# The product with v ahead of the sinks' transposes in the bank that they share

## The chip, the cores and the metric

The kernel runs on one core of a Trainium2 chip. The metric is the device time of one execution in microseconds (us). A difference is read as a ratio of medians of several runs.

## What is computed

Sliding-window attention with a few "sink" keys, a LayerNorm with a two-layer network behind it, and a token-mixing stage. Two batches, 8 heads, 768 positions, head width 64; the window is 128 keys and the first 4 keys are sinks.

```python
scores = scale * np.matmul(q, k.transpose(0, 1, 3, 2))
keep = is_sink | in_window                       # pos < n_sink, or 0 <= rel < window
scores = np.where(keep, scores, -1000000000.0)
a = np.exp(scores - np.max(scores, axis=-1, keepdims=True))
a = a / (np.sum(a, axis=-1, keepdims=True) + 1e-09)
attn = np.matmul(a, v)
...
xn = (x - mu) / np.sqrt(var + 1e-06) * g_ln
x = x + np.maximum(xn @ w_ch1, 0.0) @ w_ch2
...
theta = x @ w_theta
y = einsum('ts,bsd->btd', w_tok_r, x * cos(theta)) + einsum('ts,bsd->btd', w_tok_i, x * sin(theta))
u = x + y
out = u + np.maximum(u @ w_ch, 0.0)
```

## The kernel before

The 1536 positions of both batches are cut into six pieces of 256 (two tiles of 128 rows). Pieces 0 to 2 are batch 0, pieces 3 to 5 batch 1. Attention goes piece by piece and head by head; the network (`first`, line L625, and `second`, line L651) goes in 56 units, each for one slice of 128 hidden columns and for the one or two pieces that are active then. The work of TensorE (PE) is issued exactly in the order in which the program writes it; the other engines' instructions are put in order by the scheduler of the language, which also places the waits. `run` writes the network's units and calls `advance` between their parts, which takes the next few steps of the attention generator `attn_fast`. So PE's one queue holds parts of the network with attention steps between them, and none of it can be passed by another.

One step of `attn_fast` (one head of one piece) writes on PE, in this order:

- the scores of both tiles, each into a bank of its own (L274, L275 or L278); behind them VectorE (DVE) adds the mask (L381) and ScalarE (ACT) takes the exponential (L384), into the tile `p`;
- `turn_w` (L397), for the head one step back: three or four 128x128 transposes of `p` into a bank `wp`, which ACT (L400) and DVE (L401) read out as the two fp16 parts of `wt`;
- `finish`, which takes one more bank, named `pv`, for two unrelated things. `turn_sinks` (L410) transposes the 16 sink columns of the head that `turn_w` has just turned into columns 256 to 511; ACT (L411) and DVE (L412) read them out as the two parts of the tile `ws`. `values` (L426) multiplies the `wt` and `ws` of the head before that with v into columns 0 to 127, and DVE (L441, `normalize`) reads the result into `x`.

The sinks are turned only for pieces that do not begin a batch: 1, 2, 4 and 5, so in 32 of the 48 steps. The `ws` that `values` reads was written one whole step earlier (three `ws` tiles go round). During most of the attention the banks go round among three, and a step takes four, so a bank comes back after three more tiles.

Names in what follows: `h` is the bank of `first`, `hh` (ACT, L629) and `hl` (DVE, L630) its two parts; `acc` are the banks of `second`; `wh` (ACT, L593) and `wl` (GpSimd, POOL, L594) the parts of a weight; `xn` the normalised rows and `tp` (L571) their transposes at the end of a piece; L502 to L506 unpack the 64-bit weights.

Of the kernel before, what the change touches and what calls it, by code (L numbers as in the profile page):

```python
# [71 lines left out]
class Net:  # L72
# [207 lines left out]
    def attn_fast(self, eng):  # L280

        steps = [(piece, h) for piece in range(NP) for h in range(H)]
        nc, p, qk, pending, turned, late = self.nc, self.att, {}, [], [], []

        def load(j, eng=eng):
            if j < len(steps):
                piece, h = steps[j]
                if piece >= STACKED:
                    qk[piece, h] = self.stack_qk(piece, h, nc.gpsimd)
                elif h % 2 == 0:  # L290
                    qk[piece, h] = qk[piece, h + 1] = self.split_qk(piece, h // 2, eng)

        def load_v(piece):
            if piece < NP:
                b, tiles = self.tiles(piece)
                for t in tiles + ([NT] if tiles[-1] >= 2 else []):
                    self.split_v(b, t)

        def first_of_all(piece):
            return self.ahead() if piece == 0 else ExitStack()  # L300

        def turn():

            piece, h, pt, st = pending.pop(0)
            b, tiles = self.tiles(piece)
            with first_of_all(piece):
                wt, blocks = self.turn_w(pt, tiles)
            p["ws"].append(p["ws"].pop(0))
            turned.append((piece, h, wt, p["ws"][-1], blocks, st))
            return (pt, p["ws"][-1]) if tiles[0] else None  # L310

        def finish(sinks, ready):

            bank = self.bank("pv")
            if sinks:
                self.turn_sinks(bank, *sinks)
            if not ready:
                return
            piece, h, wt, ws, blocks, st = turned.pop(0)
            b, tiles = self.tiles(piece)  # L320
            with first_of_all(piece):
                self.values(bank, b, h, tiles, piece, wt, ws, blocks, st)
                if h % (H // 2) == H // 2 - 1:
                    self.stats(piece, h // (H // 2))
            if h == V_RANGE:
                while late:
                    q, ts = self.tiles(late.pop())
                    for t in ts:
                        with self.behind():
                            self.range_v(q, t)  # L330
            if h == H - 1:
                with first_of_all(piece):
                    self.norm(piece)
                late.append(piece)

        load(0, self.nc.vector)
        load_v(0)
        for j, (piece, h) in enumerate(steps + [(NP, 0)] * (TURN + LAG)):
            if j < len(steps):
                b, tiles = self.tiles(piece)  # L340
                if h == 0:
                    self.x[piece] = self.xp.tile([128, PIECE, DM], F32, tag=f"x{piece}", name=f"x{piece}")
                if piece < STACKED:
                    load(j + 2)
                if piece >= STACKED or h == H - 1 and piece + 1 == STACKED:
                    load(j + 1)
                if h == (3 if piece else V_NEXT):
                    load_v(piece + 1)
                pt, st = yield from self.softmax(h, tiles, qk[piece, h])
                pending.append((piece, h, pt, st))  # L350
            sinks = None
            if len(pending) > (TURN if j < len(steps) else 0):
                sinks = turn()
                yield
            ready = len(turned) > (LAG if j < len(steps) + TURN else 0)
            if sinks or ready:
                finish(sinks, ready)
                yield
        for t in tiles:
            self.range_v(b, t)  # L360
# [51 lines left out]
        nc.vector.scalar_tensor_tensor(out=ws[32:32 + NSK], in0=ps, scalar=PSC, in1=ws[0:NSK], op0=ALU.mult,  # L412
                                       op1=ALU.subtract)

    def values(self, pv, b, h, tiles, piece, wt, ws, blocks, st):

        nc = self.nc
        hc = slice(h * D, (h + 1) * D)
        for i in range(len(tiles)):
            prods = [(wt[:, x + e * len(blocks)], v[:, hc]) for e in range(2) for x, (j, t) in enumerate(blocks) if j == i  # L420
                     for v in self.v3[b, t][:2 - e]]
            if tiles[0]:
                vk = self.v3[b, NT]
                prods += [(ws[0:32 + NSK, i], vk[0:32 + NSK, 0, hc]), (ws[0:NSK, i], vk[0:NSK, 1, hc])]
            for j, (a, m) in enumerate(prods):
                nc.tensor.matmul(pv[:, i * D:(i + 1) * D], a, m, start=j == 0, stop=j == len(prods) - 1)  # L426
        self.normalize(h, pv, st, self.x[piece])

    def tiles(self, piece):
# [616 lines left out]
```

## Time and profile before

| | us |
|---|---|
| median of 3 runs (lowest to highest) | 755.43 (754.74 to 755.86) |
| the profiled execution, whole | 753.02 |
| its span in the profile | 751.2 |
| PE busy (matmuls) | 650.8 |
| DVE, ACT, POOL busy | 367.9, 365.6, 273.8 |

The profiled execution is 2.4 us shorter than the median, and 1.8 us of it lie outside the span. Attention is spread over the first 447 us of the span; from there to the end only the network's rest and the token mixing are left. A row of the trace gives what an engine did, for how long, and in brackets how long the engine had been idle before it and whose signal ended that.

### The profile page before, as it was taken

How to read it: one execution, taken by the hardware profiler on the slowest of the kernel's cores; microseconds unless marked ns; L12 is line 12 of the kernel's file. 1: busy time of each engine (PE TensorE's matmuls, PEld its weight loads, DVE VectorE, ACT ScalarE, POOL GpSimd, SP SyncE). 2: the span in 40 equal slices, each digit the busy share in tenths (PEclk: the TensorE clock that was granted, in tenths of full speed). 3: DMA queues.
4: the chain of work that ended last, by engine and by line, in shares of the span. 5: the costliest groups of instructions: out<-in, count | busy, mean ns of one | idle time of the engine just before them, and what ended most of it. 6: DMA issues, size and time to landing. Idle time of an engine off the chain costs nothing.

```text
span 751.2 us, 10135 instructions
## 1 busy us (share of the span) xinstructions
PE 650.8 (87%) x3747; PEld 523.7 (70%) x3747; DVE 367.9 (49%) x808; ACT 365.6 (49%) x774; POOL 273.8 (36%) x240
## 2 busy tenths in 40 slices
PE   3845898789889997889888889999989989899996
PEld 2633556666667675666656667778878988899996
DVE  5889624432335434353333434321367878874442
ACT  5798724344445563444434425643456656552220
POOL 3143102422437585444354117654402343330000
PEclk9999758778999998989989969999999999999999
DMA  6587401100211131110110011310011232200102
GB/s 242 185 312 262 176 20 32 30 16 0 60 31 52 44 97 40 37 38 19 37 38 1 0 57 60 123 43 0 1 31 55 85 127 71 85 15 29 37 15 82
DMA packets 19339, 50.38 MB, mean 67 GB/s; under 512 B 2769, under 2 KB 5841, under 8 KB 19281
## 3 DMA queue, kind: packets, MB, share of 16 engines
q1 hardware_dynamic: 19280, 49.66, 19.8%
q8 instruction: 31, 0.51, 0.3%
q14 instruction: 28, 0.22, 0.1%
HBM read 46.50 MB, written 3.15 MB: 66 GB/s over the span
## 4 chain that ended last, share of the span: by engine, by line
PE 38%; DVE 6%; ACT 3%; issue 1%; POOL 1%; DMA 1%; ACTq 0%; POOLq 0%; DVEq 0%
PE m L736 11%; PE h L625 8%; PE acc L651 7%; PE f L767 4%; PE th L695 4%; PE pv L426 1%; DVE st L506 1%; DVE hl L630 1%; DVE st L502 1%; DMA raw<-wtok 1%; PE tp L680 1%; DVE k L705 1%; ACT hh L629 0%; PE s L275 0%; DMA raw<-wth 0%
## 5 line engine op out<-in xcount | busy, mean ns | idle before, releaser
L594 POOL TENSOR_TENSOR wl<-w,wh 128x512 fp32r<-128x512 f32 x92 | 119.6, 1304 | 176.2 <-ACT wh L593 105.4
L625 PE MATMUL h<-xT,wh 128*128 128x512 f32 (+1 forms) x408 | 115.1, 419 | 7.6 <-DVE hl L630 7.6
L593 ACT ACTIVATE wh<-w 128x512 fp32r<-128x512 f32 x102 | 63.9, 628 | 111.0 <-PE acc L651 66.3
L625 PEld LDWEIGHTS h<-xT,wh 128*128 128x128 f32 x408 | 75.0, 210 | 27.0 <-DVE hl L630 11.2
L426 PE MATMUL pv<-v,wt 128*128 128x64 f16 x528 | 33.3, 206 | 64.9 <-DVE ws L412 55.7
L381 DVE CUSTOM_DVE_ANT_0 p<-s,mask 128x272 f32<-128x272 f32 (+1 forms) x96 | 39.4, 414 | 99.4 <-PE s L275 59.5
L651 PE MATMUL acc<-wh,hh 128*128 128x512 f32 x182 | 80.2, 441 | 0.0
L426 PEld LDWEIGHTS <-wt 128*128 128x128 f16 x528 | 26.4, 105 | 76.9 <-issue 69.0
L651 PE MATMUL acc<-wh,hl 128*128 128x512 f32 x182 | 75.1, 412 | 0.0
L651 PE MATMUL acc<-wl,hh 128*128 128x512 f32 x182 | 74.3, 408 | 0.0
L384 ACT ACTIVATE p<-p,st 128x272 f32<-128x272 f32 (+1 forms) x96 | 47.4, 494 | 51.4 <-DVE st L381 51.2
L630 DVE SCALAR_TENSOR_TENSOR hl<-h,hh 128x512 fp32r<-128x512 f32 (+1 forms) x51 | 32.1, 630 | 63.7 <-ACT hh L629 63.7
L625 PE MATMUL h<-xT,wl 128*128 128x512 f32 (+1 forms) x204 | 54.8, 394 | 0.0
L625 PEld LDWEIGHTS h<-xT,wl 128*128 128x128 f32 x204 | 39.8, 208 | 7.9
L722 POOL TENSOR_TENSOR x<-xh,xl 128x512 f32<-128x512 f32 x12 | 19.0, 1582 | 72.0 <-DVE r L716 67.2
L401 DVE SCALAR_TENSOR_TENSOR wt<-wp,wt 128x512 f16<-128x512 f32 (+1 forms) x48 | 30.7, 641 | 24.1 <-ACT wt L400 24.0
L651 PEld LDWEIGHTS acc<-wh,hl 128*128 128x128 f32 x182 | 35.9, 197 | 8.4
L651 PEld LDWEIGHTS acc<-wh,hh 128*128 128x128 f32 x182 | 35.7, 196 | 8.4
L503 ACT ACTIVATE raw<-raw 128x512 f32<-128x512 f32 (+1 forms) x52 | 36.8, 720 | 8.7 <-DVE st L502 7.6
L651 PEld LDWEIGHTS acc<-wl,hh 128*128 128x128 f32 x182 | 36.1, 198 | 5.3
L234 POOL TENSOR_TENSOR lo<-raw,hi 128x672 fp32r<-128x672 f32 (+1 forms) x11 | 18.2, 1658 | 56.4 <-ACT hi L233 56.3
L397 PE MATMUL wp<-ident,p 128*128 128x128 f32 x176 | 34.8, 322 | 2.0 <-ACT p L384 1.1
(291 smaller groups left out, 1611.2 us busy)
## 6 DMA issues: line engine op xcount, KB each, us to landing
raw<-w SPq DMA_DIRECT2D x32, 512.0 KB, 5.0
raw<-wtok SPq DMA_DIRECT2D x12, 768.0 KB, 4.2
raw<-qk SPq DMA_DIRECT2D x32, 168.0 KB, 3.0
vr<-vt SPq DMA_DIRECT2D x14, 256.0 KB, 2.7
out_dram<-o SPq DMA_DIRECT2D x24, 128.0 KB, 1.7
raw<-qk SPq DMA_DIRECT2D x20, 136.0 KB, 2.7
raw<-qk SPq DMA_DIRECT2D x8, 336.0 KB, 3.4
raw<-wth SPq DMA_DIRECT2D x4, 512.0 KB, 3.2
```

The costliest lines, as they stand in the source:

```text
L381: self.newest = [nc.vector.tensor_tensor_reduce(out=e, in0=ps[:, c0:WIN], in1=self.mask[min(t, 2)], scale=-0.125, scalar=3e38, op0=ALU.add ...
L384: nc.scalar.activation(e, e, AF.Exp, bias=st[:, 0, i:i + 1], scale=-1.0, accum_out=st[:, 1, i:i + 1])]
L397: nc.tensor.transpose(ps[:, x * 128:(x + 1) * 128], pt[:, i, c0:c0 + 128], self.ident)
L401: nc.vector.scalar_tensor_tensor(out=wt[:, m:2 * m], in0=ps, scalar=PSC, in1=wt[:, 0:m], op0=ALU.mult, op1=ALU.subtract)
L426: nc.tensor.matmul(pv[:, i * D:(i + 1) * D], a, m, start=j == 0, stop=j == len(prods) - 1)
L503: nc.scalar.activation(hi.bitcast(F32), hi.bitcast(F32), AF.Copy, scale=2.0 ** -112)
L593: nc.scalar.activation(hi, r, AF.Copy)
L594: (nc.vector if u >= UNITS - 5 else nc.gpsimd).tensor_tensor(out=lo, in0=r, in1=hi.bitcast(F32), op=ALU.subtract)
L625: nc.tensor.matmul(ps[:, 0:n], a[:, k * 128:(k + 1) * 128], x[:, k, c], start=m == 0, stop=m == 11)
L630: nc.vector.scalar_tensor_tensor(out=hl, in0=ps[:, 0:n], scalar=0.0, in1=hh.bitcast(F32), op0=ALU.max, op1=ALU.subtract)
L651: nc.tensor.matmul(ps, a[:, c], w, start=m == 0 and n == 0, stop=m == NF - 1 and n == len(prods) - 1)
L736: nc.tensor.matmul(ps, z[i][e][:, c * 128:(c + 1) * 128], w[:, t], start=s == 0 and m == 0 and c % 2 == 0, stop=s == NT - 1 and m == 5 and ...
```

## The change

In `finish` the sinks' transposes no longer come first. They are handed to `values`, which issues them behind its last product and ahead of `normalize`. Where there is no product to make (the first step of an attention run), they are issued alone as before. No operation, tile, bank or size changes.

```diff
         def finish(sinks, ready):
             bank = self.bank("pv")
-            if sinks:
-                self.turn_sinks(bank, *sinks)
             if not ready:
-                return
+                return self.turn_sinks(bank, *sinks)
             piece, h, wt, ws, blocks, st = turned.pop(0)
...
-                self.values(bank, b, h, tiles, piece, wt, ws, blocks, st)
+                self.values(bank, b, h, tiles, piece, wt, ws, blocks, st, sinks)
...
-    def values(self, pv, b, h, tiles, piece, wt, ws, blocks, st):
+    def values(self, pv, b, h, tiles, piece, wt, ws, blocks, st, sinks):
...
                 nc.tensor.matmul(pv[:, i * D:(i + 1) * D], a, m, start=j == 0, stop=j == len(prods) - 1)
+        if sinks:
+            self.turn_sinks(pv, *sinks)
         self.normalize(h, pv, st, self.x[piece])
```

Lines behind the edit move by two: L397, L401, L410, L412 and L426 of before are L395, L399, L408, L410 and L424 of the changed kernel.

PE, 28th of the 32 steps with sinks (piece 5, head 3 turned, head 2 multiplied), before; `h` is the network, `wp` the turned `p`:

```order
L397 MATMUL wp<-ident,p 128x128 x4
L625 MATMUL h<-xT,wh 128x512 x4
L625 MATMUL h<-xT,wl 128x512 x4
L410 MATMUL pv<-ident,p 16x128 x2
L426 LDWEIGHTS wt
L426 MATMUL pv<-v,wt 128x64
```

The two transposes (L410) stand between the network and the first of the sixteen products. The same place on PE, with the change, up to the first product:

```order
L395 MATMUL wp<-ident,p 128x128 x4
L625 MATMUL h<-xT,wh 128x512 x4
L625 MATMUL h<-xT,wl 128x512 x4
L424 LDWEIGHTS wt
L424 MATMUL pv<-v,wt 128x64
```

The first product now follows the network directly. And PE at the end of the same sixteen products, with the change:

```order
L424 MATMUL pv<-v,wt 128x64
L424 LDWEIGHTS ws_151
L424 MATMUL pv<-vk,ws_151 128x64
L408 MATMUL pv<-ident,p 16x128 x2
L651 MATMUL acc<-wh,hh 128x512
```

The transposes stand behind the last product now, and the network's `second` behind them. DVE at the same step, before, with the engines that each instruction waits for:

```order
L401 SCALAR_TENSOR_TENSOR wt<-wp,wt 128x512 [waits Activation_49]
L436 RECIPROCAL st<-st 128x2 [waits Activation_49]
L630 SCALAR_TENSOR_TENSOR hl<-h,hh 128x512 [waits DVE_49,Activation_49]
L412 SCALAR_TENSOR_TENSOR ws_152<-pv,ws_152 16x256 [waits Activation_49]
L441 TENSOR_TENSOR x_3238<-pv,st 128x2x64 [waits DVE_49,PE_49]
```

`normalize` (L441) stands behind the sinks' read-out and waits for PE besides. DVE at the same step with the change:

```order
L399 SCALAR_TENSOR_TENSOR wt<-wp,wt 128x512 [waits Activation_49]
L436 RECIPROCAL st<-st 128x2 [waits Activation_49]
L630 SCALAR_TENSOR_TENSOR hl<-h,hh 128x512 [waits DVE_49,Activation_49]
L410 SCALAR_TENSOR_TENSOR ws_152<-pv,ws_152 16x256 [waits Activation_49]
L441 TENSOR_TENSOR x_3238<-pv,st 128x2x64 [waits DVE_49]
```

The order is the same, and L441 has no wait for PE of its own any more. DVE at the first step with sinks (about 48 to 56 us of the trace), before; `w_...` are weights that come in from memory, `x_175` is piece 0:

```order
L502 TENSOR_SCALAR w_1046<-raw 128x512
L401 SCALAR_TENSOR_TENSOR wt<-wp,wt 128x512
L412 SCALAR_TENSOR_TENSOR ws_153<-pv,ws_153 16x256
L502 TENSOR_SCALAR w_1053<-raw 128x512
L506 SCALAR_TENSOR_TENSOR w_945<-raw,w_945 128x512
L441 TENSOR_TENSOR x_175<-pv,st 128x2x64
```

Two weight instructions stand between the sinks and `normalize`. With the change:

```order
L502 TENSOR_SCALAR w_1046<-raw 128x512
L399 SCALAR_TENSOR_TENSOR wt<-wp,wt 128x512
L502 TENSOR_SCALAR w_1053<-raw 128x512
L410 SCALAR_TENSOR_TENSOR ws_153<-pv,ws_153 16x256
L441 TENSOR_TENSOR x_175<-pv,st 128x2x64
```

`normalize` has moved up to directly behind the sinks, and one weight instruction ahead of them.

## Rows read from the trace of the kernel before

**Rows 1.** The page: busy share in 40 slices, and the granted clock.

```profile
PE   3845898789889997889888889999989989899996
PEclk9999758778999998989989969999999999999999
```

**Rows 2.** Instructions of tile ws (min/median/max ns, first and last start), and who waited.

```profile
L411 ACT ACTIVATE ws<-pv x32: 356/357/373, 50.1 to 441.5; 16x256 f16<-16x256 f32 x32
L412 DVE SCALAR_TENSOR_TENSOR ws<-pv,ws x32: 412/414/415, 54.3 to 442.3; 16x256 f16<-16x256 f32 x32
...
  PE pv L426: 55.7, 32
```

**Rows 3.** Who PE waited for, 64 to 451 us: total us, times, longest us.

```profile
PE pv L426 <- DVE ws L412: 47.8, 31, 5.6
PE h L625 <- DVE hl L630: 3.0, 3, 1.1
PE h L605 <- ACT hh L607: 2.4, 1, 2.4
PE tp L571 <- DVE xn L554: 2.3, 1, 2.3
```

**Rows 4.** Timeline, 28th step with sinks: start us, us, engine, line [idle before <-releaser].

```profile
399.52 0.38 PE L410 MATMUL pv<-ident,p 128*16 128x128 f32 x2
...
400.21 0.36 ACT L411 ACTIVATE ws<-pv 16x256 f16<-16x256 f32 x1
400.34 0.69 DVE L630 SCALAR_TENSOR_TENSOR hl<-h,hh 128x512 fp32r<-128x512 f32 x1 [1.00 <-ACT hh L629]
...
401.07 0.41 DVE L412 SCALAR_TENSOR_TENSOR ws<-pv,ws 16x256 f16<-16x256 f32 x1
...
401.53 0.34 PE L426 MATMUL pv<-v,wt 128*128 128x64 f16 x6 [1.64 <-DVE ws L412]
...
402.71 0.29 DVE L441 TENSOR_TENSOR x<-pv,st 128x128 f32<-128x128 f32 x1 [1.23 <-PE pv L426]
...
402.94 0.39 PE L651 MATMUL acc<-wl,hh 128*128 128x512 f32 x1
403.18 0.40 PE L651 MATMUL acc<-wh,hl 128*128 128x512 f32 x1
```

**Rows 5.** By stretch: length, busy (x count) of PE PEld DVE ACT POOL, clock, DMA.

```profile
50.00:64.00 14.00, 3.77 (x21) 3.00 (x21) 12.57 (x28) 13.01 (x29) 7.20 (x6) 1.00 0.72 250
...
64.00:223.00 159.00, 132.92 (x657) 94.21 (x657) 66.22 (x175) 72.73 (x176) 44.27 (x41) 0.81 0.19 63
223.00:285.00 62.00, 60.34 (x334) 45.19 (x333) 28.10 (x83) 36.75 (x93) 44.25 (x44) 1.00 0.20 59
285.00:451.00 166.00, 141.38 (x742) 102.51 (x742) 62.12 (x168) 67.54 (x164) 64.51 (x60) 0.88 0.10 30
```

**Rows 6.** Timeline, 53 to 66 us: the first two steps with sinks.

```profile
53.57 0.67 DVE L401 SCALAR_TENSOR_TENSOR wt<-wp,wt 128x512 f16<-128x512 f32 x1
...
54.74 0.64 PE L426 MATMUL pv<-v,wt 128*128 128x64 f16 x9 [7.91 <-DVE ws L412]
...
55.66 0.28 DVE L441 TENSOR_TENSOR x<-pv,st 128x128 f32<-128x128 f32 x1
...
64.10 0.48 PE L426 MATMUL pv<-v,wt 128*128 128x64 f16 x6 [5.59 <-DVE ws L412]
...
65.03 0.88 DVE L554 TENSOR_SCALAR xn<-xn,rs 128x512 f32<-128x512 f32 x2
...
65.66 1.94 PE L571 MATMUL tp<-ident,xn 128*128 128x128 f32 x8
```

**Rows 7.** Timeline of PE, 379 to 383 us: the 26th step and what follows.

```profile
379.88 0.34 PE L426 MATMUL pv<-v,wt 128*128 128x64 f16 x6 [2.50 <-DVE ws L412]
...
382.26 0.63 PE L651 MATMUL acc<-wh,hl 128*128 128x512 f32 x1
382.68 0.63 PE L651 MATMUL acc<-wh,hh 128*128 128x512 f32 x1
```

## The prediction

> **What bounds the kernel now.** I read the page first, then who waits for whom, then one step in order of time, and last the kernel by stretches. In the page [rows 1] PE is busy for eight tenths or more of nearly every slice from the 5th of 40 on, and over the stretches from 64 us on it is far ahead of every other engine [rows 5], so PE's single queue sets the time once the loading at the start is over. The question is then only what PE idles for and how fast it runs. From 64 to 451 us, where attention and the network share PE, it waits for one thing above all: the first product of `values` for the DVE half of the sinks' read-out, 47.8 us in 31 waits; the next three in the table are 3.0, 2.4 and 2.3 us [rows 3]. Over the whole kernel this wait is 55.7 us in 32 cases, one for every step with sinks [rows 2].
>
> One step shows why [rows 4]. The transposes (0.38 us) start at 399.52. ACT reads them from 400.21 to 400.57; DVE is at `hl` until 401.03 and reads them from 401.07 to 401.48; only at 401.53 does the first product start, after 1.64 us of idle PE. The products do not need this `ws` (theirs was written a step, some 9 us, earlier). They are held because they write the bank from which the sinks are being read.
>
> The second view is the clock. It is 0.81 from 64 to 223 us and 0.88 from 285 to 451 us, but 1.00 from 223 to 285 us [rows 5]. That middle stretch belongs to piece 3, which begins a batch and turns no sinks; PE is busy there for 60.34 of 62.00 us. The low readings are a mix of two levels, 2.4 and 1.2 GHz: in [rows 7], after an idle of 2.50 us, two products of `second` start 0.42 us apart, and in [rows 4] the same kind starts 0.24 us apart.
>
> **The change, part by part.** No operation is added or taken away; 64 small transposes and their 32 + 32 read-outs change place.
>
> *The wait of 30 steps.* The program's order puts the products directly behind the network's part, so their wait for this `ws` is gone, and nothing else that they need is late: `wt` and `ws` are a step old, and the bank's last reader is three tiles back. Of the 55.7 us I set the first two steps aside (7.91 and 5.59 us [rows 6]), since another engine bounds there. The rest is 55.7 - 7.91 - 5.59 = 42.2 us in 30 steps, 1.41 us each, all of it idle time in a queue that nothing can pass. I take 42.2.
>
> *The first two steps.* From 50 to 64 us DVE is busy for 12.57 and ACT for 13.01 of 14.00 us, while PE works for 3.77 [rows 5]. If PE stops waiting for `ws` it waits a little later, for `xn`: the transposes `tp` at 65.66 follow `xn` at 65.03 [rows 6], and that hangs on DVE's queue, which has the same work to do. What moves is `normalize` of piece 0, which comes directly behind `ws` and not two instructions later: it started at 55.66, and `ws` was read by about 54.7 (the product it released started at 54.74 [rows 6]). That is 1 us. Bounds: 0 and 13.5 us; I take 1, being nearest to the row that sets the end there.
>
> *The clock.* The share of time at the low level is twice what the clock lacks to 1: 2 x 0.19 x 159 = 60 us and 2 x 0.12 x 166 = 40 us [rows 5], 100 us in all. In such time about a sixth is idle (47.8 us of waits in 387 [rows 3] make an eighth, and the waits gather there), so some 84 us are work that takes 42 us at the upper level. Bounds: 0 and 42 us. The one row without the wait, 223 to 285 us, has no low level at all, though transposes, short products and scores are mixed into it too. But a step with sinks keeps more short work than a step of piece 3, namely the transposes and the products with `ws`, and part of the first stretch has other waits (2.4 and 2.3 us [rows 3]). So I take two thirds: 28 us.
>
> *What comes late next.* The engines behind PE get less time. In 223 to 285 us PE runs nearly without a break, and DVE (28.10), ACT (36.75) and POOL (44.25 of 62.00 us) keep up [rows 5]; PE idles there for 1.7 us in all. At that rate the remaining 325 us (159 + 166) would idle for about 9 us, and the 7.7 us of other waits that already stand there [rows 3] are mostly that. Where a cover goes: in [rows 4] `hl` is done at 401.03. The products (about 1.1 us, 401.53 to 402.71 less the step to DVE) and the transposes would now end at 399.52 + 1.1 + 0.38 = 401.0, and `second` with six products 0.24 us apart stands between that and the next use of the bank of `h`. So 1.4 us or more are left there. `normalize`, too, now waits for transposes and both read-outs, 0.38 + 0.36 + 0.41 = 1.15 us behind its products, but these start 1.64 us sooner. ACT and DVE meet the transposes later in their queues by the products' 1.1 us; behind the read-out on DVE stands `normalize`, and on ACT the next exponential or weight part, both with a step's lead. I take 6 us of new waits; bounds 0 and 21, half of what is removed.
>
> The rule that speaks against the change is one of the bank. The row: each of 32 products waits for the reader of other columns of its bank, 256 to 511 against 0 to 127 [rows 2]. The Trainium skill, "PSUM — Partial Sum Buffer", section "PSUM bank collisions raise a hardware error", has it that two engines must be kept apart by bank and not by address; by that rule the guard cannot vanish but turns round, and stands between the transposes and `normalize`. That is the second rival below.
>
> *Sum.* 753.0 - 42.2 - 1 - 28 + 6 = 687.8 us for the profiled execution; that one lies 2.4 us below the median of the runs, so 690 us.
>
> **The rivals.**
>
> - *The clock stays low.* The fall comes from the short products and transposes, which all remain, and not from the idle time. For it: every step with sinks has both, the idle time and the short work, and the rows don't part them. Against it: none in 62 us of piece 3. Time: 690 + 28 = 718 us.
> - *The guard turns round.* Every `normalize` comes 1.15 us later after its products, and with it DVE's queue, and PE meets that at the next transposes of `p`, which take the bank again. Price at most 30 x 1.15 = 34.5 us in place of my 6: 690 + 34.5 - 6 = 719 us. Against it: three tiles and parts of the network lie between.
> - *All of it comes back.* All waits, those of the first two steps too, the whole clock, nothing new: 753.0 - 42.2 - 13.5 - 42 + 2.4 = 658 us. Against it: DVE and ACT are full in the first 64 us.
> - *Nothing changes.* The products still wait for a `ws`, their own of the step before: 755 us. It would need a read-out a whole step late; it takes 0.36 and 0.41 us [rows 2].
> - *Slower.* Place: the bank of `h`, one for all units. Where `hl` is queued on DVE behind `ws` and `normalize`, PE's next `first` waits for transposes, both read-outs, `normalize` and `hl`: 0.38 + 0.36 + 0.41 + 0.29 + 0.69 = 2.13 us, and some 0.2 us for the hand-overs. If that stood bare in all 32 steps it would cost 75 us against a gain of 42.2 + 1 + 28 = 71: 4 us slower, about 759. It decides only from 2.2 us per step on. Against it: `hl` stands ahead of `ws` in the order shown.
>
> **How the numbers follow.** Forecast (690, in itself 675 to 706 by the bounds of clock and new waits) 0.60; the clock stays 0.14; the guard turns round 0.12; all of it 0.08; nothing changes 0.03; slower 0.03. The range from 667 to 720 takes in the forecast, the two slower ways of gaining and part of the 658 case, and leaves out under 2 in 10. A difference below 0.2% (1.5 us) can't be told from none in this kernel. Faster: 0.60 + 0.14 + 0.12 + 0.08 = 0.94; same 0.03; slower 0.03.
>
> **What would show it.** The wait of the products for the sinks' read-out should be gone from PE's table (47.8 us to under 2). `normalize` should start right behind DVE's read-out, with no wait for PE. The clock over the stretches with sinks should rise from 0.81 and 0.88 to about 0.95. The last read-out of sinks, now at 442.3 us [rows 2], should come near 380. The 300 us from 451 to the end of the span should stay as they are. I am wrong if PE's waits for `hl`, `wt` or `p` grow to more than 20 us, if the clock keeps below 0.9 there, or if `tp` of piece 0 (65.66 us [rows 6]) moves by more than 3 us.

## The result, and the profile after

The changed kernel takes 677.19 us (median of 4 runs, 676.15 to 680.61) against 755.09 us (4 runs of the kernel before beside it): ratio 0.900, 95% interval 0.892 to 0.908. The forecast was 690 us with a range from 667 to 720; the time is 13 us below the forecast and within the range. The kernel before scatters by some 2% with its granted clock (0.924 to 0.950 in the runs of the experiments below), and not by the 0.2% that the first three runs had suggested; hence the width of the intervals. The profiled execution is 676.33 us, 76.7 us below that of before (753.02).

The page of the changed kernel, busy time and granted clock in 40 slices of a span that is 76.8 us shorter:

```profile
PE 610.5 (91%) x3747; PEld 499.0 (74%) x3747; DVE 367.8 (55%) x808; ACT 365.2 (54%) x774; POOL 275.3 (41%) x240
PE   3772799699999999999999998999899898999996
PEclk9999999799999999999999998999899898999999
```

DVE and ACT do the same work to 0.4 us (367.9 and 365.6 before). PE does the same 3747 products in 610.5 busy us and not 650.8: it also runs faster. Against [rows 1] every reading below 9 in the first half of the clock's line is gone but one. Four 8s stand now between the 25th and the 34th slice, where attention is over; before, all slices behind it read 9.

Who PE waited for from 64 to 370.4 us (total us, times, longest us), to be held against [rows 3]. The last product of attention now ends at 366.7 us, before at 447.2, so each window ends 3.7 or 3.8 us behind it:

```profile
PE tp L571 <- DVE xn L554: 14.2, 2, 9.1
PE h L605 <- ACT hh L607: 3.5, 1, 3.5
PE h L625 <- DVE hl L630: 3.3, 3, 1.2
PE h L605 <- ACT raw L503: 1.2, 1, 1.2
```

The products' wait for the sinks' read-out is not in the table any more. Over the whole kernel one such wait is left of the 32 with 55.7 us [rows 2]:

```profile
PE pv L424 <- DVE ws L410: 0.5, 1, 0.5
```

It is no longer a wait for the bank: in the second step the products need the `ws` of the first step for themselves.

The 28th step, that of [rows 4], in order of time (start, us, engine, line, idle before and its releaser):

```profile
332.15 0.35 PE L424 MATMUL pv<-v,wt 128*128 128x64 f16 x6
...
332.98 0.69 DVE L630 SCALAR_TENSOR_TENSOR hl<-h,hh 128x512 fp32r<-128x512 f32 x1 [1.00 <-ACT hh L629]
333.24 0.39 PE L408 MATMUL pv<-ident,p 128*16 128x128 f32 x2
333.38 0.49 PE L651 MATMUL acc<-wh,hh 128*128 128x512 f32 x1
333.66 0.37 ACT L409 ACTIVATE ws<-pv 16x256 f16<-16x256 f32 x1 [0.71 <-PE pv L408]
...
334.06 0.41 DVE L410 SCALAR_TENSOR_TENSOR ws<-pv,ws 16x256 f16<-16x256 f32 x1 [0.40 <-ACT ws L409]
...
334.51 0.29 DVE L441 TENSOR_TENSOR x<-pv,st 128x128 f32<-128x128 f32 x1
```

PE goes from the products to the transposes and on to the network without a gap. The waits are now on ACT (0.71 us) and DVE (0.40 us), which have time for them, and `normalize` follows the read-out at once.

By stretch (length, busy and count of PE, PEld, DVE, ACT, POOL, granted clock, DMA). The bounds follow the work, as in [rows 5]: piece 3 now lies at 188 to 245.6 us.

```profile
64.00:188.00 124.00, 112.39 (x666) 81.73 (x666) 67.28 (x178) 75.38 (x183) 47.13 (x44) 0.97 0.26 83
188.00:245.60 57.60, 56.45 (x320) 42.56 (x320) 26.33 (x78) 34.47 (x86) 41.55 (x42) 1.00 0.23 64
245.60:370.40 124.80, 121.84 (x739) 90.00 (x739) 58.97 (x167) 67.06 (x163) 64.40 (x59) 1.00 0.12 35
```

The clock is 0.97 and 1.00 where it was 0.81 and 0.88 [rows 5]. By the same reckoning as before, 2 x 0.03 x 124 = 7 us at the lower level are left of 100.

From the last product of attention to the end of the span, before and with the change:

```profile
447.20:751.20 304.00, 287.34 (x1852) 259.39 (x1851) 164.48 (x245) 139.18 (x223) 99.80 (x68) 0.98 0.16 55
366.70:674.40 307.70, 289.18 (x1851) 261.35 (x1851) 167.98 (x247) 140.03 (x225) 99.81 (x68) 0.97 0.16 55
```

Attention is done 80.5 us earlier, and the same work behind it takes 3.7 us more. PE waits longer there for `hl` (7.5 us and not 4.7), and its clock is a little lower.

### The profile page after: what moved, and what is told of

Read it like the earlier page. It is cut to its first block, busy times and chain, and to the rows that moved or that the text cites. A ratio compares the mean times of both kernels' runs of the same rounds, so it can differ in the third digit from the quotient of the medians.

```text
span 674.4 us, 10138 instructions
## 1 busy us (share of the span) xinstructions
PE 610.5 (91%) x3747; PEld 499.0 (74%) x3747; DVE 367.8 (55%) x808; ACT 365.2 (54%) x774; POOL 275.3 (41%) x240
## 4 chain that ended last, share of the span: by engine, by line
PE 75%; DVE 10%; ACT 6%; DMA 5%; POOL 2%; issue 2%; SPq 0%; ACTq 0%; POOLq 0%; DVEq 0%
PE acc L651 18%; PE h L625 17%; PE m L736 12%; PE f L767 5%; PE pv L424 5%; PE th L695 4%; PE s L278 3%; PE wp L395 3%; DMA raw<-w 2%; PE s L275 2%; DMA raw<-wtok 2%; PE h L605 1%; PE pv L408 1%; DVE w L502 1%; DVE w L506 1%
## 5 line engine op out<-in xcount | busy, mean ns | idle before, releaser
L625 PE MATMUL h<-xT,wh 128*128 128x512 f32 (+1 forms) x408 | 104.6, 389 | 10.0 <-DVE hl L630 10.0
L593 ACT ACTIVATE wh<-w 128x512 fp32r<-128x512 f32 x102 | 63.9, 628 | 70.5 <-PE acc L651 44.9
L625 PEld LDWEIGHTS h<-xT,wh 128*128 128x128 f32 x408 | 69.1, 193 | 26.3 <-DVE hl L630 13.0
L651 PE MATMUL acc<-wh,hh 128*128 128x512 f32 x182 | 77.5, 426 | 0.0
L651 PE MATMUL acc<-wh,hl 128*128 128x512 f32 x182 | 72.3, 397 | 0.8 <-DVE hl L630 0.8
L651 PE MATMUL acc<-wl,hh 128*128 128x512 f32 x182 | 72.0, 395 | 0.0
L625 PE MATMUL h<-xT,wl 128*128 128x512 f32 (+1 forms) x204 | 50.6, 370 | 0.0
L424 PE MATMUL pv<-v,wt 128*128 128x64 f16 x528 | 32.7, 202 | 13.0 <-DVE wt L399 7.1
L424 PEld LDWEIGHTS <-wt 128*128 128x128 f16 x528 | 24.0, 103 | 25.2 <-issue 11.3
L399 DVE SCALAR_TENSOR_TENSOR wt<-wp,wt 128x512 f16<-128x512 f32 (+1 forms) x48 | 30.8, 641 | 19.9 <-ACT wt L398 19.8
L625 PEld LDWEIGHTS h<-xT,wl 128*128 128x128 f32 x204 | 36.5, 191 | 6.7
L395 PE MATMUL wp<-ident,p 128*128 128x128 f32 x176 | 33.0, 309 | 2.0 <-ACT p L382 1.0
```

The lines of the kernel that those rows point to most:

```text
L395: nc.tensor.transpose(ps[:, x * 128:(x + 1) * 128], pt[:, i, c0:c0 + 128], self.ident)
L593: nc.scalar.activation(hi, r, AF.Copy)
L625: nc.tensor.matmul(ps[:, 0:n], a[:, k * 128:(k + 1) * 128], x[:, k, c], start=m == 0, stop=m == 11)
L651: nc.tensor.matmul(ps, a[:, c], w, start=m == 0 and n == 0, stop=m == NF - 1 and n == len(prods) - 1)
```

## The experiments

The theory: PE waited because the products write the bank from which ACT and DVE read the sinks; the idle time also cost the clock, and both come back with the change. The rivals: it is the place in PE's queue that counts and not the bank; the clock is low for the short work and not for the idle time; the gain is not made step by step; the late `normalize` now costs what the guard cost before. Each experiment was timed against the kernel before on its own chip, so ratios are compared and not times. The medians of the kernel before in the three sets were 754.21, 758.09 and 753.53 us.

### The sinks in a bank of their own

```diff
-            bank = self.bank("pv")
             if sinks:
-                self.turn_sinks(bank, *sinks)
+                self.turn_sinks(self.bank("sk"), *sinks)
             if not ready:
                 return
+            bank = self.bank("pv")
```

> The kernel before, with the sinks' transposes still ahead of the products, but in a bank of their own, so that no bank is shared. Theory (the products wait for the readers of their bank): the wait of 55.7 us is gone in spite of the old order, the clock rises as in the changed kernel, and the time is 677 to 695 us; a step now takes five tiles of three banks, so some new waits of PE for an earlier reader are allowed for. Rival (it is the place in PE's queue that counts, the sinks being read late by busy engines): the wait stays and the time is about 755 us.

Measured 679.48 us, ratio 0.901 (0.894 to 0.908): the gain of the change, in the old order. PE's timeline at the 28th step of this kernel:

```profile
336.60 0.38 PE L410 MATMUL sk<-ident,p 128*16 128x128 f32 x2
336.81 0.34 PE L426 MATMUL pv<-v,wt 128*128 128x64 f16 x6
```

The transposes stand first as before, and the products follow 0.21 us after their start, with no idle time noted. So it was the shared bank that held the products, and not their place in the queue nor a late read-out. The waits are placed by the scheduler of the language, and each of these banks is also one tile of the program; no run parts the bank from the tile.

### The change in one batch

The guard of before is put back for one half of the steps (here for the second batch; the other experiment has `<` for `>=`):

```diff
             if not ready:
                 return self.turn_sinks(bank, *sinks)
+            if sinks and turned[0][0] >= NP // 2:
+                self.turn_sinks(bank, *sinks)
+                sinks = None
```

> The change in the first batch alone (16 of 32 steps; in the second batch the transposes come first again). Theory (each step gives back its own wait and the clock that it cost, on the spot): by the starts of the transposes in the two traces the first batch gave 39 of the 77 us, so 716 us (710 to 722), and the wait of the products in the other 16 steps stays at about 23 us. Rival (the gain of one batch is taken back or brought about by the other): under 700 or over 735 us.

> The change in the second batch alone (the other 16 of 32 steps). Theory (each step gives back its own wait and the clock that it cost): the two halves add up. The first batch alone gave about 43 of the 77 us, so this gives 34 +- 5: 720 us (715 to 726), with some 32 us of the products' wait left in the first batch. Rival (the halves help one another, or one half lifts the clock for all): under 710 or over 735 us.

Measured for the first batch alone 711.12 us, ratio 0.942 (0.934 to 0.950), and for the second alone 719.75 us, ratio 0.950 (0.946 to 0.954). The losses of time, 5.8% and 5.0%, add up to 10.8%; the whole change takes 10.0% (9.2 to 10.8). Against the kernel before on their own chips they gave 43 us (39 expected) and 38 us (34 +- 5 expected). The wait that is left (23 and 32 us expected), first with the change in batch 0, then in batch 1 (lines moved by one):

```profile
PE pv L427 <- DVE ws L413: 23.4, 17, 2.5
```

```profile
PE pv L427 <- DVE ws L413: 35.0, 16, 7.8
```

Each half keeps its own waits. The clock by stretch, first with the change in batch 0, then in batch 1:

```profile
64.00:188.70 124.70, 112.37 (x666) 81.81 (x666) 67.53 (x178) 75.33 (x183) 47.12 (x44) 0.93 0.26 83
...
246.10:407.40 161.30, 136.59 (x750) 99.90 (x750) 61.74 (x168) 67.63 (x165) 65.68 (x60) 0.93 0.10 31
```

```profile
64.00:229.00 165.00, 136.84 (x654) 96.58 (x652) 66.81 (x174) 72.61 (x175) 44.08 (x41) 0.78 0.18 60
...
291.70:416.50 124.80, 121.83 (x739) 90.09 (x738) 59.02 (x167) 67.13 (x162) 64.39 (x59) 1.00 0.12 35
```

With the change in batch 1 alone the clock parts sharply, 0.78 in the unchanged half and 1.00 in the changed one. With the change in batch 0 alone it does not: 0.93 in both, though the unchanged half read 0.88 before. The lengths are clearer. The changed half takes 124.7 us against 159 and, in the other kernel, 124.8 us against 166, as in the kernel with the whole change (124.0 and 124.8 us); the unchanged half takes 161.3 us against 166, or 165.0 against 159. So each half gives back its own time, but for the 5 or 6 us by which an unchanged half itself differs from profile to profile.

### Work in the place of the idle time

The order of before, and between transposes and products something for PE to do that nobody reads: one product of 128x512, or eight 128x128 transposes of about the same length.

```diff
                 self.turn_sinks(bank, *sinks)
             if not ready:
                 return
+            if sinks:
+                fill = self.bank("fill")
+                nc.tensor.matmul(fill, self.ident, self.gain, start=True, stop=True)
```

```diff
-                nc.tensor.matmul(fill, self.ident, self.gain, start=True, stop=True)
+                for i in range(8):
+                    nc.tensor.transpose(fill[:, i % 4 * 128:(i % 4 + 1) * 128], self.ident, self.ident)
```

> The kernel before with one more product (identity by 128x512 fp32, 0.87 us at the upper clock) written between the sinks' transposes and the products, into a bank of the round that nobody reads. The wait stays as long as it was, less the filler, and PE's work grows by 28 us. Theory (the idle time costs the clock): the clock from 64 to 223 and 285 to 451 us rises from 0.81 and 0.88 to over 0.94 and the time falls to 715 to 735 us though nothing waits less long for the sinks. Rival (the short products and transposes cost the clock): clock as before, time 755 us or some us over.

> The kernel before with a filler again in the place of the idle time, but eight 128x128 transposes (0.87 us at the upper clock) instead of the one long product. If it is only idle time that costs the clock, it does what the product did: 725 us (718 to 732), clock of the whole about 0.97. If short work such as transposes costs the clock as idle time does, the clock stays near 0.93 and the time at 750 us or over.

Measured 725.13 us with the product, ratio 0.961 (0.953 to 0.970), and 727.03 us with the transposes, ratio 0.959 (0.954 to 0.964). PE does some 30 us more work (32 times 0.9 to 1.0 us) and the kernel is some 30 us faster. The step with the product, in order of time:

```profile
384.60 0.38 PE L413 MATMUL pv<-ident,p 128*16 128x128 f32 x2
...
384.82 1.02 PE L321 MATMUL fill<-gain,ident 128*128 128x512 f32 x2
...
386.15 0.41 DVE L415 SCALAR_TENSOR_TENSOR ws<-pv,ws 16x256 f16<-16x256 f32 x1
...
386.62 0.34 PE L429 MATMUL pv<-v,wt 128*128 128x64 f16 x6 [0.78 <-DVE ws L415]
```

The products still wait for the read-out, from 384.98 (start of the transposes and their 0.38 us) to 386.62, 1.64 us as in [rows 4]; only 0.78 of it is idle. With the product, and then with the transposes, by stretch (the two parts with sinks):

```profile
64.00:205.40 141.40, 123.87 (x690) 85.06 (x690) 68.81 (x177) 74.03 (x180) 45.56 (x42) 0.93 0.21 71
...
265.90:421.00 155.10, 142.39 (x781) 99.08 (x780) 61.50 (x168) 67.21 (x164) 65.58 (x60) 0.98 0.11 32
```

```profile
64.00:210.00 146.00, 127.62 (x769) 94.96 (x769) 68.14 (x176) 73.61 (x178) 44.50 (x41) 0.89 0.21 69
...
272.30:427.60 155.30, 142.77 (x873) 108.54 (x872) 61.54 (x168) 67.21 (x164) 65.58 (x60) 0.98 0.11 32
```

The clock rises from 0.81 and 0.88 to 0.93 and 0.98, or to 0.89 and 0.98. So it was the idle time that had cost the clock. Short work did not: added transposes raised it. The product was expected to bring both stretches over 0.94, and the first just missed it; the transposes were expected to bring the whole to about 0.97, and it is 0.966. That they reach only 0.89 in the first stretch proves little in one profile each.

### `normalize` ahead of the transposes

```diff
+        self.normalize(h, pv, st, self.x[piece])
         if sinks:
             self.turn_sinks(pv, *sinks)
-        self.normalize(h, pv, st, self.x[piece])
```

> The changed kernel with normalize written ahead of the transposes (products, normalize, transposes). Theory (the guard of the bank stands wherever two engines follow one another in it): now the transposes, and all of PE's queue behind them, wait for DVE's normalize, at least 0.1 + 0.29 + 0.06 = 0.45 us in 32 steps, more where DVE is busy: 14 to 40 us over the changed kernel, 691 to 717 us, still well below 755. Rival (the late normalize is what the changed kernel suffers from): below 677 us.

Measured 690.75 us, ratio 0.914 (0.907 to 0.921). Who PE waited for, and a step in order of time:

```profile
PE pv L408 <- DVE x L441: 19.4, 32, 3.6
```

```profile
341.03 0.29 DVE L441 TENSOR_TENSOR x<-pv,st 128x128 f32<-128x128 f32 x1 [0.91 <-PE pv L424]
341.37 0.39 PE L408 MATMUL pv<-ident,p 128*16 128x128 f32 x2 [0.38 <-DVE x L441]
```

The guard has turned round: now the transposes wait in all 32 steps, for a reader of other columns of the bank, 0.6 us each. This is the rule of the Trainium skill that the prediction named ("PSUM — Partial Sum Buffer", section "PSUM bank collisions raise a hardware error": engines are kept apart by bank and not by address), and the rows agree with it from both sides, 32 waits of 55.7 us in one order [rows 2] and 32 of 19.4 us in the other. In the order of the change the guard stands before `normalize`, on an engine that has time. The time lies at the lower end of what was expected. By the ratios, 0.914 against 0.900, this order costs about 10 us; the two intervals just touch.

### Piece 1 earlier

The changed kernel has one wait that grew: `tp` for piece 1 waits 5.14 us for the normalised rows, 2.3 us before [rows 3], and the clock falls behind it.

```profile
127.39 0.88 DVE L554 TENSOR_SCALAR xn<-xn,rs 128x512 f32<-128x512 f32 x2 [0.58 <-POOL rs L548]
128.03 1.08 PE L571 MATMUL tp<-ident,xn 128*128 128x128 f32 x4 [5.14 <-DVE xn L554]
128.76 0.78 PE L651 MATMUL acc<-wh,hh 128*128 128x512 f32 x1
...
129.34 0.63 PE L651 MATMUL acc<-wl,hh 128*128 128x512 f32 x1
129.76 0.63 PE L651 MATMUL acc<-wh,hl 128*128 128x512 f32 x1
```

The products behind it start 0.42 us apart, the lower level of [rows 7]. The number `READY1` says by which unit of the network the attention of piece 1 must be done.

```diff
-READY1 = 6.5
+READY1 = 5.5
```

> The changed kernel with the attention of piece 1 a whole unit of the network earlier (READY1 5.5 for 6.5), for the wait of 5.1 us for the normalised rows of piece 1 that the changed kernel has at 128 us, with the low clock of 6.8 us behind it. If that wait is on the path: 5.1 us and up to 3.4 us of clock less, 669 to 673 us. If the network of one piece is too thin to cover attention that comes closer together, the waits for wt and hl in the first 120 us take it back: 677 us or over.

> As the one before, two units earlier (READY1 4.5). If one unit was not enough to hide the wait, this is 2 us or so below it; if attention that comes closer together costs, it is above it: 668 to 685 us.

> The kernel before with READY1 5.5 for 6.5, nothing else. If the 8 us that this number gave on the changed kernel came from a wait that the change made (the normalised rows of piece 1, 2.3 us before and 5.1 us after), it gives a third to a half of it here or nothing: 751 to 757 us. If it is a gain of its own that the change has no part in, 747 us.

Measured on the changed kernel 668.87 us with 5.5 (ratio to the kernel before 0.884, 0.881 to 0.888) and 669.53 us with 4.5 (0.884, 0.880 to 0.889). That is faster than both kernels, by some 1.8% against the change alone (0.900): the intervals lie clear of that one. The wait is gone; of the two for `tp` only the one at the start of the network is left:

```profile
PE tp L571 <- DVE xn L554: 9.3, 1, 9.3
```

The last run decided for the second of its two readings. The same number on the kernel before gives 745.63 against 753.53 us, ratio 0.987 (0.980 to 0.995): a gain of 1.3%, small, but its interval lies clear of none. Within their intervals the two gains are alike, so most of it is a gain of its own that the change has no part in; a small share of the change is not excluded. The wait in the kernel before was only 2.3 us there (0.7 us are left), so more than the wait comes back. The trace shows where the rest lies: PE does the same products in less time (650.8 us busy before), that is, at a higher clock (0.941 over the whole and not 0.928).

```profile
PE 642.2 (86%) x3747; PEld 519.5 (70%) x3747; DVE 371.1 (50%) x808; ACT 365.3 (49%) x774; POOL 274.6 (37%) x240
```

In one profile of a kernel whose clock scatters as this one's does, it stays open how much of these 8.6 us belongs to the number.

## Why the prediction was right, point by point

*The 30 steps*, 42.2 us: right. The waits are gone (32 to one of 0.5 us), and the experiment with a bank of its own shows that the shared bank was their cause.

*The first two steps*, 1 us of 13.5: right in kind, nearly nothing in size. PE now waits elsewhere in them, for `wt` and 9.11 us for `xn`, and `tp` starts at 65.81 us (65.66 before [rows 6]). `normalize` did move up, to 54.99 from 55.66, but the rows of `xn` were ready no sooner:

```profile
54.21 0.29 PE L424 MATMUL pv<-v,wt 128*128 128x64 f16 x2 [2.83 <-DVE wt L399]
...
65.81 1.94 PE L571 MATMUL tp<-ident,xn 128*128 128x128 f32 x8 [9.11 <-DVE xn L554]
```

*What comes late next*, 6 us: right in size, and that in part by luck. PE's idle time in the whole span went from 751.2 - 650.8 = 100.4 us to 674.4 - 610.5 = 63.9 us, so by 36.5 us; against 42.2 us that is 5.7 us of new waits. In the stretch that the term was worked out for they are fewer: PE's other waits from 64 us to the end of attention (table above, less the 9.1 us that belong to the first two steps) are 5.1 + 3.5 + 3.3 + 1.2 = 13.1 us, before 3.0 + 2.4 + 2.3 + 1.5 = 9.2 us (the last is one wait of `first` for DVE at L577). That is 3.9 us more. The rest came behind attention, where nothing was to change. The cover that was named held: in the 28th step `hl` is done at 333.67, and `second` is then still at work.

*The clock*, 28 us: too small, and this term makes the whole miss. PE did the same products in 650.8 - 610.5 = 40.3 us less, near the upper bound of 42; with the 36.5 us of idle time these are the 76.8 us of the span. The step that failed is the two thirds: the short work that stays in a step with sinks was held to keep a third of the low level, and it keeps hardly any. The stretch of piece 3, which had no low level at all [rows 5], was the better guide than the reserve against it. The filled kernels show the term by itself, some 30 us with half of the idle time still there (28.4 of 55.7 us with the product).

*The landmarks.* The last read-out of the sinks was expected near 380 us and starts at 364.7 us, 77.6 us earlier than before (442.3 [rows 2]). The last 300 us did not stay quite as they were: from the last product of attention on they take 307.7 us and not 304.0. The kernels with a bank of their own and with the change in batch 1 need 307.2 and 308.1 us there, so this small loss is not one profile's chance. The clock came to 0.97 and 1.00, not to 0.95. Of the signs of being wrong none came; `tp` of piece 0 moved by 0.15 us.

*The rivals.* "The clock stays low" and "nothing changes" are out by the profile after. "The guard turns round" is right as a mechanism, but costs PE nothing where `normalize` is the one to wait, and 19.4 us of waits where PE is. "All of it comes back" came nearest: the clock did, the first two steps did not. "Slower" needed `hl` behind the read-out; PE's waits for `hl` up to the end of attention went from 3.0 to 3.3 us.

## What to carry to other kernels

In this kernel two unrelated uses of one accumulation bank were tied together even though their columns differ, so in an in-order queue write first what can be read later at leisure, and last what has to be read before the bank can be written again. Idle time of the bounding engine should be costed twice where the clock is seen to fall beside it: here 42 us of waits were worth 82 us (42.2 + 40.3) before the new waits. And a stretch of the same trace that lacks the wait is the best forecast of the clock without it.

## What the runs showed of the hardware

In each of the 30 steps counted, PE idled for 0.91 to 2.51 us in a queue that was otherwise busy, and the granted clock read 0.81 and 0.88 there: about a quarter of the time between 64 and 451 us at 1.2 GHz. With some 0.9 us of work in the place of that idle time, transposes as well as a product, the clock read 0.89 to 0.98, and with no such wait 0.97 and 1.00. The time of the kernel before also scatters more, 745.96 to 755.86 us in four runs, than that of the changed one beside it, 676.15 to 680.61 us in four.
